# Attention sums with the tails added in, a small first transfer, and a new order table

## The chip, the cores and the metric

The kernel runs on one core of a Trainium2 chip. A core has a matrix engine (PE), three elementwise engines (DVE, ACT, POOL) and a queue engine (SP) that issues nearly all transfers; each executes its own list of instructions in order and waits for the others through semaphores. The metric is the device time of one execution in microseconds (us). Everything is float32 to the reference's accuracy, which is why one product is often made of three.

## The reference

Four batches of 12 heads, 448 positions, head size 64; then a gated block whose width is 768.

```python
scores = (q @ k.T) / 8
scores = cap * tanh(scores / cap)
attn   = softmax(scores)              # + 1e-9 in the denominator
x      = attn @ v                     # heads side by side: [4, 448, 768]
h      = gelu(x @ w_in)               # 768 -> 1024, tanh form
u, v   = h[..., :512], h[..., 512:]
v      = layernorm(v) * g_ln
v_s    = w_sg @ v + b_sg              # over the 448 positions
out    = x + (u * v_s) @ w_out        # 512 -> 768
```

## The kernel before

**Attention.** Two heads make a *pair* (24 pairs, 6 per batch, input pairs `q2[b, p]` and `k2[b, p]` of 128 rows by 448 columns), and two pairs make a *group* (12 groups, three per batch). The 448 keys are three chunks of 128 and a tail of 64. So a group has seven *units*: pair 0 with key chunks 1, 2, 3, pair 1 with chunks 1, 2, 3, and one unit that holds the tails of both pairs. One unit does, in this order:

- its scores on PE, for two heads at once. A chunk's scores (line 548) use the pair split in a high and a low half: `hl` is made by a cast (line 331 on DVE or 333 on ACT) and a subtraction (DVE, line 361), both 896 columns wide, and three products of the halves are added. The tail's scores (line 556) and the very first unit's (line 562, `whole`) take the raw float32 inputs and need no split;
- tanh and exp on ACT (lines 617 and 619, 896 columns each), in a tile `p`;
- values on PE (line 576, the tail's 586) into the pair's sums in PSUM;
- denominators: a matmul with columns of ones adds `p` over the keys into `den` (line 493, at most two units in one step). In a group whose entry in `SUMS` is 0 each of the seven units goes there. Where it is 1, DVE first adds the three chunks of a pair (line 636, 896 columns), so that two sums and the tail unit are left: three in place of seven.

Per batch a reciprocal follows through DRAM (lines 643 to 666), and the pairs' results are scaled and split again for the gated block.

**Gated block**, once per batch, on PE: `hv` (line 756, 18 matmuls for each 128 positions, three or four such blocks), `hu` (line 796, four blocks of 18), `vsg` (line 813, four blocks of 11), `outp` (line 834, six blocks of 12). Each block ends in one PSUM bank, and two banks at most are held by them at a time (`G_CAP`). The gelu of a block is Square on ACT (737), a step on DVE (739), Tanh on ACT (742), a step on DVE (744); the second step frees the bank.

**Weights** come as 64-bit numbers and are taken apart on DVE (lines 415 to 430), put together by POOL (line 435), then split in two halves (331 or 333, and 361). This is done for 12 chunks of `w_in` and 8 of `w_out`, and fills DVE early in the program.

**The order.** Nothing is ordered by hand. Each operation has a key from tables at the top (`ATT`, `GATED`, `IN_V`, `SPLIT`, `NORM`, ...), and `Plan.run` simulates five engines with fixed costs and takes, for each engine, the ready operation with the smallest key (a change of kind of matmul on PE is charged with `SWITCH`). Buffers are pools (`SIZES`). What comes out is a fixed list per engine.

Of the kernel before, what the change touches and what calls it, by code (L numbers as in the profile page):

```python
# [8 lines left out]
FP32 = mybir.dt.float32  # L9
# [13 lines left out]
ATT = ((-72.86, 2.67), (-7.76, 2.13), (126.82, 7.56), (80.49, -23.95))  # L23
GATED = ((141.52, 109.73), (434.23, 29.43), (324.93, 194.27), (407.54, 133.09))
SWITCH = 338.54
SIZES = (3, 6, 4, 4, 14, 2)
# [8 lines left out]
RETIRE = (12, 12, 11, 12, 0, 0)
IN_V = (418.5, 26.3)
IN_U = (73.7, 77.4)
OUT_W = (67.1, 53.5)
SG_W = (1690.2, 26.3)
FETCH_W = 222.3  # L40
FETCH_G = 41.72
SPLIT = 63.86
SG_FETCH = (349.8, 62.0)
GELU = 320.1
NORM = 231.27
RECIP = 518.42
VAL = 45.43
DEN = 46.86
DEC_AHEAD = 258.5
# [205 lines left out]
def kernel(  # L255
# [10 lines left out]
    consts: bass.AP,  # L266
    outT: bass.AP,
# [77 lines left out]
    k_const, k_bsg, k_g, k_pw = (Buf() for _ in range(4))  # L345
# [18 lines left out]
    load(lambda: const_sb, consts, k_const, 80000, -98.7)  # L364
# [8 lines left out]
    op("dve", 0.5, prepare, rd=[k_const], wr=[k_guard], key=1.0)  # L373
# [5 lines left out]
    def warm():  # L379

        z, o = Buf(p_p), Buf(ps_p, cls="w")
        op("dve", 0.3, lambda: nc.vector.memset(z.t[:, 0, :256], 0.0), wr=[z], key=-99.0)

        def fn():
            for _ in range(WARM):
                nc.tensor.matmul(
                    out=o.t[:, :256], lhsT=z.t[:, 0, :128], rhs=z.t[:, 0, :256], start=True, stop=True)
        op("pe", WARM * mms(4, 256, sets=1), fn, rd=[z], wr=[o], key=-99.0, mode="G")
# [91 lines left out]
    def attention(b):  # L480
# [3 lines left out]
        total = sum(3 if s else NU for s in SUMS[NG * b:NG * b + NG])  # L484
# [22 lines left out]
        def group(gi):  # L507
            g = NG * b + gi
            i0 = NU * g
# [21 lines left out]
            def split(s):  # L531
                key = akey(i0 + (FC + 1) * s) - SPLIT
                parts = range(2) if g == 0 and s == 0 else (slice(0, 2),)
                for n in parts:
                    cols = S if isinstance(n, int) else 2 * S
                    reg = n if isinstance(n, int) else None
                    cop(lambda n=n: hl[s].t[:, 0, n], lambda n=n: raw[s].t[:, n], cols,
                        [(raw[s], reg)], [(hl[s], ("h", n) if reg is not None else "h")], key)
                    sub(lambda n=n: hl[s].t[:, 1, n], lambda n=n: raw[s].t[:, n], lambda n=n: f32(hl[s].t[:, 0, n]), cols,
                        [(raw[s], reg), (hl[s], ("h", n) if reg is not None else "h")],  # L540
                        [(hl[s], ("l", n) if reg is not None else "l")], key)

            def scores(i, s, c, sc):
                def fn():
# [7 lines left out]
                def tail():  # L552
                    for s in range(2):
                        for h in range(2):
# [3 lines left out]
                                rhs=raw[s].t[rows, 0], start=True, stop=True, skip_group_check=True)  # L558
                def whole():
                    for h in range(2):  # L560
                        rows = slice(64 * h, 64 * h + 64)
                        nc.tensor.matmul(
                            out=sc.t[:, h, :S], lhsT=raw[s].t[rows, 1, 128 * c - 128:128 * c],
                            rhs=raw[s].t[rows, 0], start=True, stop=True)

                if c == 1 and s == 0 and not g:
# [370 lines left out]
```

## Time and profile before

| what | before |
|---|---|
| three runs | 391.77 us median (388.27 to 392.88) |
| the profiled execution | 390.62 us, of which the span of instructions is 388.2 us |
| PE busy | 377.8 us, 97% of the span |
| DVE busy | 288.4 us, 74% |
| ACT busy | 232.8 us, 60% |
| PE idle, or without work, at the two ends | until 4.0 us, and from 384.5 us |

The shares are averages. The first 109 us hold batches 0 and 1 of attention, the first units of batch 2 and the decoding of `w_in`; from there on the gated blocks alternate with the rest of attention; the last 112 us are gated work alone.

### The profile page before, as it was taken

The page shows a single profiled execution, that of the slowest core. Times are in us where ns is not written, and L with a number is a line of the kernel's source. Part 1 is how long each engine was busy: PE and PEld are TensorE (multiplying, and loading weights), DVE is VectorE, ACT ScalarE, POOL GpSimd, SP SyncE. Part 2 cuts the span into 40 slices and gives each one's busy share as a digit, 9 for nine tenths or more (in the row PEclk, how much of TensorE's full clock was granted, in tenths as well). Part 3 has the DMA queues.
Part 4 walks back from the last instruction along what each step waited for, and adds up shares of the span by engine and source line. Part 5 has one row for each costly group of instructions (what it writes and reads, how often), then busy time and mean ns, then how long its engine had stood idle before and what let it go on. Part 6 is the DMA issues. An engine that isn't in the chain of part 4 may idle for free.

```text
span 388.2 us, 5669 instructions
## 1 busy us (share of the span) xinstructions
PE 377.8 (97%) x2112; PEld 252.7 (65%) x2112; DVE 288.4 (74%) x521; ACT 232.8 (60%) x313; POOL 46.5 (12%) x38
## 2 busy tenths in 40 slices
PE   6998999999999999999999999999999999999996
PEld 3433433434788475888965844445689889889995
DVE  3699999799999999837656574878377797365642
ACT  5998999998456896714347399987134413133200
POOL 0261023046231310201000000000010000010000
PEclk9999999999999999999999999999999999999999
DMA  8981752864253533420004114322121201100012
GB/s 254 333 284 35 245 179 64 243 207 165 54 130 112 160 94 104 163 94 0 2 0 122 49 41 134 101 96 95 34 54 49 71 24 61 59 0 2 1 71 95
DMA packets 26155, 39.59 MB, mean 102 GB/s; under 512 B 5809, under 2 KB 23569, under 8 KB 26129
## 3 DMA queue, kind: packets, MB, share of 16 engines
q1 hardware_dynamic: 25984, 39.13, 32.0%
q8 instruction: 16, 0.26, 0.3%
q10 hardware_dynamic: 144, 0.11, 0.1%
q14 instruction: 11, 0.08, 0.1%
HBM read 33.21 MB, written 6.02 MB: 101 GB/s over the span
## 4 chain that ended last, share of the span: by engine, by line
PE 72%; DVE 15%; DMA 6%; ACT 2%; issue 2%; SPq 1%; POOL 0%; DVEq 0%; ACTq 0%; POOLq 0%
PE ps L796 11%; PE ps L576 10%; PE ps L756 9%; PE sc L548 8%; PE ps L834 8%; PE ps L813 6%; PE sc L834 4%; PE sc L796 4%; PE den L493 4%; PE sc L756 3%; DVE hl L361 2%; PE sc L813 2%; PE ps L586 2%; DMA n<-spread 2%; PE sc L556 2%
## 5 line engine op out<-in xcount | busy, mean ns | idle before, releaser
L617 ACT ACTIVATE p<-sc,qsc 128x896 f32<-128x896 f32 x84 | 81.3, 1019 | 10.7 <-DVE p L636 4.2
L619 ACT ACTIVATE p<-p,const_sb 128x896 f32<-128x896 f32 x84 | 84.0, 1059 | 0.1
L576 PE MATMUL ps<-p,v 128*64 128x448 f32 x288 | 61.2, 550 | 0.2 <-ACT p L619 0.2
L548 PEld LDWEIGHTS sc<-hl 64*128 64x128 f32 x426 | 35.9, 184 | 38.4 <-ACT p L617 19.8
L548 PE MATMUL sc<-hl 64*128 64x448 f32 x426 | 56.9, 388 | 2.8 <-ACT p L617 2.4
L435 POOL TENSOR_TENSOR stage<-stage 128x512 int32<-128x512 int32 (+1 forms) x20 | 38.3, 1918 | 112.5 <-DVE stage L430 111.1
L756 PE MATMUL ps<-win,rg 128*128 128x512 f32 x188 | 45.2, 395 | 0.0
L796 PE MATMUL ps<-rg,win 128*128 128x448 f32 x206 | 44.0, 365 | 0.0
L834 PE MATMUL ps<-rg,wout 128*128 128x448 f32 x184 | 43.4, 368 | 0.2
L636 DVE TENSOR_TENSOR p<-p,p 128x896 f32<-128x896 f32 x36 | 39.0, 1085 | 5.5 <-PE ps L576 3.1
L756 PEld LDWEIGHTS ps<-win,rg 128*128 128x128 f32 x188 | 35.3, 188 | 8.5
L796 PEld LDWEIGHTS ps<-rg,win 128*128 128x128 f32 x206 | 38.6, 187 | 3.4
L576 PEld LDWEIGHTS ps<-p,v 128*64 128x64 f32 x288 | 17.6, 136 | 34.2 <-issue 23.0
L834 PEld LDWEIGHTS ps<-rg,wout 128*128 128x128 f32 x184 | 34.0, 188 | 4.8 <-issue 0.9
L737 ACT ACTIVATE t<-ps 128x448 f32<-128x448 f32 (+1 forms) x23 | 13.1, 568 | 37.6 <-PE ps L756 22.5
L361 DVE TENSOR_TENSOR hl<-raw,hl 128x896 fp32r<-128x896 f32 (+1 forms) x25 | 26.8, 1070 | 6.1 <-ACT hl L333 5.9
L772 POOL TENSOR_TENSOR sm<-sm,pw 128x1 f32<-128x1 f32 x14 | 8.0, 572 | 189.9 <-DVE sm L769 189.9
L742 ACT ACTIVATE t<-t 128x448 f32<-128x448 f32 (+1 forms) x30 | 18.1, 603 | 16.4 <-DVE t L739 16.3
L813 PE MATMUL ps<-wsg,rg 128*128 128x448 f32 x116 | 26.3, 369 | 0.0
L739 DVE SCALAR_TENSOR_TENSOR t<-t,ps 128x448 f32<-128x448 f32 (+1 forms) x23 | 14.9, 647 | 14.0 <-ACT t L737 13.9
L493 PE MATMUL den<-p,const_sb 128*32 128x448 f32 x192 | 24.1, 549 | 0.3 <-DVE p L636 0.3
L813 PEld LDWEIGHTS ps<-wsg,rg 128*128 128x128 f32 x116 | 21.6, 188 | 3.0 <-issue 1.0
(114 smaller groups left out, 463.8 us busy)
## 6 DMA issues: line engine op xcount, KB each, us to landing
stage<-in_w_in_dram SPq DMA_DIRECT2D x12, 512.0 KB
raw<-in_q_dram SPq DMA_DIRECT2D x24, 224.0 KB
raw<-in_k_dram SPq DMA_DIRECT2D x24, 224.0 KB
n<-spread SPq DMA_DIRECT2D x24, 224.0 KB
out_dram<-x SPq DMA_DIRECT2D x23, 224.0 KB
v<-in_vp_dram SPq DMA_DIRECT2D x24, 192.0 KB
stage<-in_w_out_dram SPq DMA_DIRECT2D x8, 384.0 KB
u<-in_w_sgT_dram SPq DMA_DIRECT2D x4, 224.0 KB
```

What stands on the lines that cost most here:

```text
L361: op("dve", c_tt(n), lambda: nc.vector.tensor_tensor(out=out(), in0=a(), in1=b(), op=ALU.subtract), rd=rd, wr=wr, key=key, fast=True)
L435: nc.gpsimd.tensor_tensor(out=a.bitcast(I32), in0=a.bitcast(I32), in1=hi, op=ALU.add)
L493: nc.tensor.matmul(out=den.t[32 * j:32 * j + 32, :S], lhsT=ones_sb[:, kind, NP - 1 - kind - p:NP + 31 - kind - p], rhs=src.t[:, h, :], sta ...
L548: nc.tensor.matmul(out=sc.t[:, h, :S], lhsT=hl[s].t[rows, w, 1, 128 * c - 128:128 * c], rhs=hl[s].t[rows, m, 0], start=(k == 0), stop=(k = ...
L576: nc.tensor.matmul(out=pav[s].t[64 * h:64 * h + 64, :S], lhsT=v[s].t[:, 128 * (c - 1) + 64 * h:128 * (c - 1) + 64 * h + 64], rhs=p.t[:, h, ...
L617: op("act", c_act(2 * S, True, True), lambda p=p, sc=sc: nc.scalar.activation(out=p.t, in_=sc.t[:, :, :S], func=ACTF.Tanh, scale=qsc), rd= ...
L619: op("act", c_act(2 * S, False, True), lambda p=p: nc.scalar.activation(out=p.t, in_=p.t, func=ACTF.Exp, scale=cap_sb), rd=[k_const], wr=[ ...
L636: op("dve", c_tt(2 * S), lambda a=a, p=p: nc.vector.tensor_tensor(out=a.t, in0=a.t, in1=p.t, op=ALU.add), rd=[p], wr=[a], key=akey(i) + 5. ...
L756: nc.tensor.matmul(out=ps.t[:, :HF], lhsT=(xl if a else xh)[c].t[:, t * 128:t * 128 + 128], rhs=win[w][:, c, HF:], start=(c == 0 and k == ...
L796: nc.tensor.matmul(out=ps.t[:, :S], lhsT=win[w][:, c, f * 128:(f + 1) * 128], rhs=(xl if a else xh)[c].t[:, :S], start=(c == 0 and k == 0) ...
L813: nc.tensor.matmul(out=ps.t[:, :S], lhsT=(vl if a else vh)[c].t[:, f * 128:(f + 1) * 128], rhs=wsg[w][:, c, :], start=(c == 0 and k == 0), ...
L834: nc.tensor.matmul(out=ps.t[:, :S], lhsT=wout[w][:, f, c * 128:(c + 1) * 128], rhs=(gl if a else gh)[f].t[:, :S], start=(f == 0 and k == 0 ...
```

## The change

1. **Sums.** `SUMS` may now be 2: the halves of the tail unit's `p` (64 rows each) are added into the two pairs' sums on DVE, with two additions of 64 rows by 896 columns, and only two units go to `den`. The last four groups get 2; group 5 goes from 0 to 1. `TPOS` puts the tail unit second in each group (fourth in group 0).
2. **Plain pairs.** A table `PLAIN` names three pairs (0 and 3 of batch 0, 0 of batch 2) whose chunks' scores are made by `whole` from raw float32, without a split.
3. **First transfer.** A new input `first` holds 128 columns of k of the first pair, and `cap`; it is loaded ahead of all else, and the first unit reads its keys there. `const_sb` loses `cap` and is loaded later.
4. **Warm-up matmuls** at the start have 208 columns (`WCOLS`) in place of 256.
5. **Order.** New numbers in all key tables and costs; five `p` tiles in place of six and 16 `x` tiles in place of 14.

```diff
-ATT = ((-72.86, 2.67), (-7.76, 2.13), (126.82, 7.56), (80.49, -23.95))
+ATT = ((-54.55, 0.66), (20.94, 1.35), (147.45, 6.3), (106.98, -9.84))
-SIZES = (3, 6, 4, 4, 14, 2)
+SIZES = (3, 5, 4, 4, 16, 2)
...
-SUMS = (0, 1, 1, 1, 0, 0, 1, 1, 1, 1, 1, 1)
+SUMS = (0, 1, 1, 1, 0, 1, 1, 1, 2, 2, 2, 2)
+PLAIN = (1, 0, 0, 1, 0, 0, 0, 0, 0, 0, 0, 0, 1, 0, 0, 0, 0, 0, 0, 0, 0, 0, 0, 0)
...
-    load(lambda: const_sb, consts, k_const, 80000, -98.7)
+    load(lambda: first_sb, first, k_first, 70000, -99.5)
+    load(lambda: const_sb, consts, k_const, 60000, -98.3)
...
-        total = sum(3 if s else NU for s in SUMS[NG * b:NG * b + NG])
+        total = sum((NU, 3, 2)[s] for s in SUMS[NG * b:NG * b + NG])
...
+                if PLAIN[NP * b + pairs[s]]:
+                    return
...
-                if c == 1 and s == 0 and not g:
-                    op("pe", mms(4, sets=1), whole, rd=[raw[s]], wr=[sc], key=akey(i), mode="F")
+                if early:
+                    op("pe", mms(4, sets=1), whole, rd=[(raw[s], 0), k_first], wr=[sc], key=akey(i), mode="S")
+                elif c and PLAIN[NP * b + pairs[s]]:
+                    op("pe", mms(4, sets=1), whole, rd=[raw[s]], wr=[sc], key=akey(i), mode="S")
...
-            units.insert(FC if g else 1, (0, 0))
+            units.insert(tpos, (0, 0))
...
+                def add(a, p, rows=slice(0, 128)):
+                    op("dve", c_tt(2 * S), lambda: nc.vector.tensor_tensor(
+                        out=a.t[rows], in0=a.t[rows], in1=p.t[rows], op=ALU.add),
+                       rd=[p], wr=[a], key=akey(i) + 5.0, fast=True)
...
+                if SUMS[g] == 2 and (c == 0 or (s, c) == (1, 1)):
+                    add(per[s], tail_p, slice(64 * s, 64 * s + 64))
+                if (s, c) == ((0, 0) if SUMS[g] == 2 and tpos == FC else (0, FC)) or (s, c) == (1, FC):
+                    den_unit(pairs[s], 0, per[s], akey(i) + DEN, last)
```

**PE at the start.** Ahead of these rows stand only the warm-up matmuls. `sc` are the two score banks, `raw` the inputs of a pair, `hl` its halves, `ps` a pair's sums, `p` the exponentials. Before (line 562 is `whole`, 556 the tail's scores, 548 the scores from the halves, 576 values):

```order
L562 MATMUL sc_126<-raw_80 128x448 x2
L556 MATMUL sc_127<-raw_80 64x448 x2
L556 MATMUL sc_127<-raw_81 64x448 x2
L548 MATMUL sc_126<-hl_83 128x448 x6
L576 MATMUL ps_129<-p_91,v_85 64x448 x2
```

The same place of the change (571 is `whole`, 563 the tail's scores, 587 values, 501 denominators):

```order
L571 MATMUL sc_128<-raw_81,first_sb 128x448 x2
L571 MATMUL sc_129<-raw_81 128x448 x2
L571 MATMUL sc_128<-raw_81 128x448 x2
L563 MATMUL sc_129<-raw_81 64x448 x2
L563 MATMUL sc_129<-raw_82 64x448 x2
L587 MATMUL ps_131<-p_92,v_86 64x448 x2
```

The three chunks of pair 0 now come first, from raw inputs, and the tails, which need both pairs, fourth; the first product from halves has moved behind values and denominators.

**DVE at the gelus of the first gated block.** These are the rows up to the second step of the second `hv` block, which frees the bank that the first `hu` block takes. `t` is a gelu tile, `ps` the bank, `stage` a weight chunk being decoded, `win` the halves of `w_in`, `d` the reciprocals of batch 1. Before:

```order
L739 SCALAR_TENSOR_TENSOR t_117<-t_117,ps_130 128x512
L425 TENSOR_SCALAR stage_78<-stage_78 128x512
L430 SCALAR_TENSOR_TENSOR stage_78<-stage_78 128x512
L657 SCALAR_TENSOR_TENSOR d_139<-d_139,guard 64x84
L744 SCALAR_TENSOR_TENSOR t_118<-t_117,ps_130 128x512
L660 RECIPROCAL d_139<-d_139 64x84
...
L739 SCALAR_TENSOR_TENSOR t_115<-t_115,ps_128 128x512
L768 BN_AGGR sm_122<-sm_122 128x2
L361 TENSOR_TENSOR win_64<-stage_78,win_63 128x512
L769 TENSOR_SCALAR sm_122<-sm_122 128x1
L361 TENSOR_TENSOR wout_66<-stage_79,wout_65 128x384
L744 SCALAR_TENSOR_TENSOR t_116<-t_115,ps_128 128x512
```

And with the change (758 and 763 are the two gelu steps, 429 to 438 the decoding):

```order
L758 SCALAR_TENSOR_TENSOR t_119<-t_119,ps_131 128x512
L368 TENSOR_TENSOR win_64<-stage_80,win_63 128x512
L676 SCALAR_TENSOR_TENSOR d_141<-d_141,guard 64x84
L763 SCALAR_TENSOR_TENSOR t_120<-t_119,ps_131 128x512
...
L758 SCALAR_TENSOR_TENSOR t_117<-t_117,ps_132 128x512
L438 SCALAR_TENSOR_TENSOR stage_79<-stage_79 128x512
L793 TENSOR_SCALAR t_120<-t_120,sm_124 128x512
L763 SCALAR_TENSOR_TENSOR t_118<-t_117,ps_132 128x512
...
L368 TENSOR_TENSOR win_64<-stage_79,win_63 128x512
```

The last subtraction of a `w_in` chunk (stage_78 before, stage_79 now) stood ahead of that second gelu step and stands behind it now; the work on a `w_out` chunk has moved out of these rows.

**PE behind the first gated block's last `hv` block.** The last rows are the block's last matmul and what follows. Before, attention of batch 2 follows (its tails and a chunk):

```order
L756 MATMUL ps_128<-win_63,rg_700 128x512
L556 MATMUL sc_127<-raw_80 64x448 x2
L556 MATMUL sc_127<-raw_81 64x448 x2
L548 MATMUL sc_126<-hl_84 128x448 x6
```

With the change nine matmuls of `vsg` (line 832) come first, the last of which is the first row here:

```order
L832 MATMUL ps_130<-wsg_67,rg_628 128x448
L587 MATMUL ps_131<-p_94,v_86 64x448 x2
L555 MATMUL sc_129<-hl_84 128x448 x6
L555 MATMUL sc_128<-hl_84 128x448 x6
```

A block of `vsg` is now begun, left in its bank, and finished after ten units of attention.

## Rows read from the trace of the kernel before

**Rows 1.** Stretches: from:to, length, busy PE, PEld, DVE, ACT, POOL (instructions), clock, DMA, GB/s
```profile
4.00:8.60 4.60, 2.98 (x15) 0.77 (x14) 2.59 (x9) 2.41 (x5) 0.00 (x0) 1.00 1.01 330
...
13.50:108.90 95.40, 92.07 (x609) 41.34 (x601) 91.73 (x156) 85.28 (x100) 30.85 (x14) 1.00 0.56 177
108.90:170.10 61.20, 61.01 (x325) 45.56 (x326) 57.49 (x118) 41.13 (x65) 9.93 (x10) 1.00 0.42 129
```

**Rows 2.** Timeline of PE: start, length, line, operands, count [idle before <-releaser]
```profile
108.86 0.48 PE L796 MATMUL ps<-r,win 128*128 128x448 f32 x1 [0.33 <-DVE t L744]
```

**Rows 3.** The chain that ended last, at that place: start, length, what
```profile
108.12 0.70 DVE t L744
...
108.86 15.12 PE ps L796 x72
```

**Rows 4.** What DVE waited for between 13.4 and 108.9 us: total, times, longest
```profile
DVE x L699 <- DMA n<-spread: 2.5, 2, 1.9
DVE stage L421 <- DMA stage<-in_w_in_dram: 2.2, 3, 1.4
```

**Rows 5.** Timeline of DVE, two places where it works back to back
```profile
83.24 0.64 DVE L331 CAST hl<-raw 128x896 fp32r<-128x896 f32 x1
83.78 0.64 DVE L361 TENSOR_TENSOR rg<-x,rg 128x448 fp32r<-128x448 f32 x1
...
97.64 1.08 DVE L361 TENSOR_TENSOR hl<-raw,hl 128x896 fp32r<-128x896 f32 x1
98.65 0.68 DVE L361 TENSOR_TENSOR win<-stage,win 128x512 fp32r<-128x512 f32 x1
99.25 1.08 DVE L636 TENSOR_TENSOR p<-p,p 128x896 f32<-128x896 f32 x1
100.25 0.41 DVE L421 TENSOR_SCALAR stage<-stage 128x512 f32<-128x512 f32 x1
```

**Rows 6.** Timelines of ACT and DVE at the start
```profile
6.65 0.95 ACT L333 ACTIVATE hl<-raw 128x896 fp32r<-128x896 f32 x1 [1.36 <-DMA raw<-in_k_dram]
7.50 0.99 ACT L617 ACTIVATE p<-sc,qsc 128x896 f32<-128x896 f32 x1
...
13.48 0.45 DVE L421 TENSOR_SCALAR stage<-stage 128x512 f32<-128x512 f32 x1 [1.40 <-DMA stage<-in_w_in_dram]
```

**Rows 7.** Timeline of PE: the first unit, then attention back to back
```profile
4.04 1.02 PE L562 MATMUL sc<-raw 64*128 64x448 f32 x4
4.99 0.97 PE L556 MATMUL sc<-raw 64*64 64x448 f32 x4
...
41.18 1.72 PE L576 MATMUL ps<-p,v 128*64 128x448 f32 x8
42.84 1.48 PE L548 MATMUL sc<-hl 64*128 64x448 f32 x12
44.25 0.98 PE L586 MATMUL ps<-p,vt 64*64 64x448 f32 x8
...
47.49 2.48 PE L576 MATMUL ps<-p,v 128*64 128x448 f32 x12
49.90 0.87 PE L548 MATMUL sc<-hl 64*128 64x448 f32 x6
50.70 0.98 PE L556 MATMUL sc<-raw 64*64 64x448 f32 x8
51.61 1.72 PE L576 MATMUL ps<-p,v 128*64 128x448 f32 x8
...
70.79 1.71 PE L493 MATMUL den<-p,const_sb 128*32 128x448 f32 x16
72.43 0.88 PE L548 MATMUL sc<-hl 64*128 64x448 f32 x6
```

**Rows 8.** Timeline of POOL
```profile
83.13 9.17 POOL L435 TENSOR_TENSOR stage<-stage 128x512 int32<-128x512 int32 x1 [17.45 <-DVE stage L430]
...
103.28 1.29 POOL L435 TENSOR_TENSOR stage<-stage 128x512 int32<-128x512 int32 x1 [7.45 <-DVE stage L430]
```

More of the change, by code (lines that the diff above doesn't have):

```diff
@@ L31 @@
 WARM = 3
-COLD = 7.0
-SHARED = {'act': 224.0, 'dve': 104.5}
-SUMS = (0, 1, 1, 1, 0, 0, 1, 1, 1, 1, 1, 1)
[L35 to L49, printed above, removed]
+WCOLS = 208
+COLD = 4.1
+SHARED = {'act': 334.0, 'dve': 134.7}
+SUMS = (0, 1, 1, 1, 0, 1, 1, 1, 2, 2, 2, 2)
+PLAIN = (1, 0, 0, 1, 0, 0, 0, 0, 0, 0, 0, 0, 1, 0, 0, 0, 0, 0, 0, 0, 0, 0, 0, 0)
+RETIRE = (11, 12, 12, 12, 0, 3)
+IN_V = (90.12, 42.36)
+IN_U = (76.43, 52.83)
+OUT_W = (448.39, 25.57)
+SG_W = (2004.62, 22.75)
+FETCH_W = 142.75
+FETCH_G = 614.08
+SPLIT = 125.16
+SG_FETCH = (156.89, 59.95)
+GELU = 309.21
+NORM = 137.72
+RECIP = 888.07
+VAL = 24.89
+DEN = 12.46
+TVAL = 32.36
+TPOS = 1
+TPOS0 = 3
+DEC_AHEAD = 198.71
 ISSUE = 0.45
@@ L266 @@
     consts: bass.AP,
+    first: bass.AP,
     outT: bass.AP,
@@ L386, in fn @@
                 nc.tensor.matmul(
-                    out=o.t[:, :256], lhsT=z.t[:, 0, :128], rhs=z.t[:, 0, :256], start=True, stop=True)
-        op("pe", WARM * mms(4, 256, sets=1), fn, rd=[z], wr=[o], key=-99.0, mode="G")
+                    out=o.t[:, :WCOLS], lhsT=z.t[:, 0, :128], rhs=z.t[:, 0, :WCOLS], start=True, stop=True)
+        op("pe", WARM * mms(4, WCOLS, sets=1), fn, rd=[z], wr=[o], key=-99.0, mode="G")
     warm()
@@ L508, in group @@
             g = NG * b + gi
+            tpos = TPOS if g else TPOS0
             i0 = NU * g
@@ L532, in split @@
                 key = akey(i0 + (FC + 1) * s) - SPLIT
[L533 to L541, printed above, removed]
+                if PLAIN[NP * b + pairs[s]]:
+                    return
+                cop(lambda: hl[s].t[:, 0], lambda: raw[s].t, 2 * S, [raw[s]], [(hl[s], "h")], key)
+                sub(lambda: hl[s].t[:, 1], lambda: raw[s].t, lambda: f32(hl[s].t[:, 0]), 2 * S,
+                    [raw[s], (hl[s], "h")], [(hl[s], "l")], key)
             def scores(i, s, c, sc):
+                early = not g and not s and c == 1
                 def fn():
@@ L578, in fn @@
                             lhsT=v[s].t[:, 128 * (c - 1) + 64 * h:128 * (c - 1) + 64 * h + 64],
-                            rhs=p.t[:, h, :], start=(s == 0 and c == 1), stop=((s == 1 or not g) and c == FC),
+                            rhs=p.t[:, h, :], start=(s == 0 and c == 1), stop=((s == 1 or tpos < FC) and c == FC),
                             skip_group_check=True)
@@ L587, in tail @@
                                 out=pav[s].t[64 * h:64 * h + 64, :S], lhsT=vtail.t[rows, 64 * h:64 * h + 64],
-                                rhs=p.t[rows, h, :], start=(s == 1), stop=(g > 0 and s == 0), skip_group_check=True)
+                                rhs=p.t[rows, h, :], start=(s == 1), stop=(tpos == FC and s == 0), skip_group_check=True)
                 if c:
@@ L591, in values @@
                 else:
-                    op("pe", mms(4, sets=1, records=8), tail, rd=[vtail, p], wr=pav, key=akey(i) + VAL, mode="Q")
+                    op("pe", mms(4, sets=1, records=8), tail, rd=[vtail, p], wr=pav, key=akey(i) + TVAL, mode="Q")
             def evac(i, s):
@@ L877 @@
         plan.run()
-_INS = ["q2", "k2", "vp", "vt", "w_in", "w_sgT", "b_sg", "w_out", "consts"]
+_INS = ["q2", "k2", "vp", "vt", "w_in", "w_sgT", "b_sg", "w_out", "consts", "first"]
 def kernel(**inputs):
```

39 lines of the change are left out of this document (21 added, 18 removed).

## The prediction

> **What bounds the kernel now.** I read the page's busy times first (in the table above): PE 97%, DVE 74%. Neither number decides, so the next view is the table of stretches, cut where the program changes its work. From 13.5 to 108.9 us DVE is busy for 91.73 of 95.40 us and PE for 92.07 [rows 1]: two engines are full at once. In the 61 us behind it DVE still has 57.49 us of work, PE 61.01.
>
> Which of the two sets the pace is told by what PE waits for at the seam. The first `hu` block begins at 108.86 after an idle 0.33 us, released by DVE's second gelu step [rows 2], and the chain that ended last enters PE there, out of DVE (108.12, line 744), to run 15.12 us through 72 matmuls [rows 3]. So at 108.86, which I call the *gate*, DVE is late and PE waits. DVE's list of waits up to there holds only transfers, 2.5 us for the broadcast reciprocals and 2.2 us for weight chunks, 1.4 of it at the very start [rows 4]. I take it that DVE from its first weight chunk at 13.48 [rows 6] to the gate is a sum of instructions, with a few us of transfers and collisions that the change doesn't touch. Behind the gate I take PE to be the bound: it has 0.2 us idle in the next 61 [rows 1].
>
> The time is then: gate, plus PE's work behind it, plus the end.
>
> **What ends at the gate: DVE.** I counted the instructions of both orders from the first decoding step to that gelu step. A price is the distance between two starts where DVE works back to back [rows 5]: subtraction of 896 columns 1.01 us (97.64 to 98.65), of 512 columns 0.60, addition of 896 columns 1.00, cast of 896 columns 0.54 (83.24 to 83.78). Half widths I take at half, 0.5 and 0.3 (estimates).
>
> - Splits: 13 subtractions and 12 casts stood there, now 10 and 9. Three pairs are plain or already split before the first chunk lands: -3.0 and -1.6.
> - Additions: 14, now 16 (group 5 has moved to sums; none of the tails' additions is this early): +2.0.
> - `w_sg` is split ahead of the gate, three chunks more, each a cast and a subtraction of 448 columns: +2.4. The work on a `w_out` chunk has moved behind it (four instructions of 384 columns, three quarters of 0.60 twice and of some 0.35 twice): -1.4. The last `w_in` subtraction has moved behind it: -0.6. A layernorm step and a cast come ahead: +0.8.
>
> Sum -1.4 us. The start of that work doesn't gain: DVE waits for the first chunk of `w_in` [rows 6], and 66 KB more now go ahead of it, at 330 GB/s [rows 1] +0.2. So the gate moves from 108.9 to 107.7, **-1.2**.
>
> **What the first transfer gains, and why I cost it at nothing.** Before, the first scores end near 5.0 [rows 7], but tanh starts at 7.50, because ACT had first to wait for the second pair's k until 6.65, and to cast it [rows 6]. The new order has no cast on ACT there, and the first scores need only the small table and one q: tanh can begin near 5.1, 2.4 us earlier. That puts ACT and PE ahead, and DVE's decoding is the cover that hides it: both arrive at the gate and wait. If DVE were not the bound it would be worth the whole 2.4 (first rival). The shorter warm-up, three matmuls of 48 columns less, is hidden in the same way.
>
> **What is left behind the gate: PE.** Prices, again from start to start [rows 7]: one more unit of values 0.75 (four records more: 1.66, then 2.41 us), entering values 0.16; a unit of chunk scores 0.61 and entering it 0.20 (1.41 for two, 0.80 for one); a tail's scores 0.91; two steps of denominators 1.64, so 0.75 for a step of two units and 0.14 to enter. The first unit took 0.95 with raw inputs against 0.80 with halves, so a plain unit costs 0.15 more; eight more of them are 1.2 us, all ahead of the gate, where PE waits anyway.
>
> Behind the gate the orders differ so: denominators 36 matmuls, now 28 (four units, two steps): -1.5. One chunk's scores -0.6 and one tail's scores -0.9, which now lie ahead of it; one unit of values more, +0.75. Changes of kind: values entered 18 times instead of 14 (+0.6), scores 20 instead of 22 (-0.4), denominators 7 instead of 8 (-0.1), gated kinds five times more, for which I have no clean row: between nothing and the 0.20 of scores, I take 0.1 (+0.5). Sum **-1.7**; with the ends of the unknown -2.2 to -1.2.
>
> The eight additions of 64 rows and four more of 128 lie on DVE mostly behind the gate. No row shows 64 rows by 896 columns; bounds are nothing and the 1.00 of 128 rows, and I take 1.00, since an instruction's length here follows its columns. PE hides them, if DVE keeps up: in the next stretch 23 units of attention now stand beside the first gated block's second half, where 11 stood, and DVE had 3.7 us to spare in 61. I leave this at nothing, with up to 3 us of new waits in the range.
>
> **Sum.** 388.2 - 1.2 - 1.7 = 385.3 us of span; 2.4 us lie around the span, so the profiled execution would be 387.7 in place of 390.62. The median of the runs shown stands 1.15 us above that execution, which gives 388.9. I predict 388.5.
>
> **Rivals.**
>
> *The start carries through* (chance 0.17). If DVE's waits for transfers vanish because denominators and reciprocals come earlier, PE decides. Its work ahead of the gate is 1.0 us more (eight raw units at 0.75 for seven from halves at 0.61, one tail unit more, two steps of denominators and one unit of values less, some changes of kind). It starts 2.4 earlier, and of the 3.3 us that it idled in that stretch (95.40 - 92.07) [rows 1] none need stay: the gate is at 104.2. Span 388.2 - 4.7 - 1.7 = 381.8, time 384.2 on the profiled execution's scale. For it: DVE waited 3.7 us in this stretch. Against it: the new list puts the same distance of work between the reciprocals and their first use.
>
> *A late chunk of `w_in`* (chance 0.10), the side on which it gets slower. The last chunk's decoding now ends about 1.1 us ahead of the gate, and its subtraction has moved behind the gate. POOL's step stands between: usually 1.29 us, but once 9.17 [rows 8]. With 1.3, a cast and the subtraction, the halves are there some 1.5 us behind the gate; `hu` asks for them after 15 matmuls, 3.2 us behind it at 0.2 each [rows 3]. So it decides from 3.0 us of POOL on. At 9.2 PE stands 6.2 us: span 391.5, time 393.9. For it: the long one ran while DVE went through subtractions and multiplications of two inputs, and such stand there now. The Trainium skill (GPSIMD Engine Reference, 1. Specifications) says why it could be so: POOL's memory interfaces are shared with VectorE, and DVE instructions with two SBUF inputs contend with it. By that rule each of this change's additions is a chance to hold POOL up; the 9.17 us agree, the 1.29 us beside other additions don't make it regular. Against it: before, even the 9 us cost PE nothing.
>
> *Nothing happens* (chance 0.13). What PE saves at denominators it waits for at additions, or DVE's order loses in collisions what its sum gains: 390.6 to 391.8.
>
> The forecast has the remaining 0.60.
>
> **Range and chances.** The unknowns of the forecast (1 us in the changes of kind, 3 of new waits, 2 or 3 of transfers and collisions) make it 386 to 391. Eight in ten needs the upper half of the first rival and nothing: 383.5 to 392.5. About 2% is what a measurement of this kernel can tell from no change, since three runs lie 1.2% apart. Faster by over 2% is below 383.9: half of the first rival and a little of the forecast, 0.11. Slower by over 2% is above 399.6, which no single mechanism here reaches: 0.02.
>
> **What would show it.** Tanh starts at 5.0 to 5.5 in place of 7.50. DVE's first decoding step stays within 0.5 us of 13.5. PE shows more waiting than before between 13 us and the gate, on DVE, and the first `hu` block begins at 107 to 108.5. From there to the last matmul PE takes about 274 us (275.6 before: 384.5 - 108.9). Were the gate below 105, DVE was no bound and the first rival holds; were it at 108 but the stretch behind it longer than 276, the additions have turned into waits; an idle PE some 3 us into the first `hu` block is the late chunk.

## The result, and the profile after

The changed kernel takes 385.91 us (median of 20 runs, 384.68 to 389.13) where the kernel before took 389.54 (387.67 to 392.88) on the same chip: a ratio of 0.9897, with a 95% interval of 0.9874 to 0.992. The prediction was 388.5 us with a range of 383.5 to 392.5, and no change beyond 2%. The profiled execution has a span of 383.6 us, before 388.2: 4.6 us less, where the prediction summed 2.9.

The busy times, from the profile's page:

```profile
PE 373.9 (97%) x2064; PEld 250.7 (65%) x2064; DVE 298.9 (78%) x533; ACT 229.7 (60%) x305; POOL 44.4 (12%) x38
```

PE has 3.9 us less to do than before, DVE 10.5 us more. The stretches, which answer to [rows 1] (from:to, length, busy PE, PEld, DVE, ACT, POOL, clock, DMA, GB/s), cut at the first `hu` block again:

```profile
4.00:8.60 4.60, 4.16 (x18) 1.49 (x20) 0.13 (x1) 3.18 (x4) 0.00 (x0) 1.00 0.97 307
13.50:108.80 95.30, 92.55 (x581) 39.89 (x580) 92.22 (x154) 85.57 (x97) 26.59 (x13) 1.00 0.59 187
108.80:170.10 61.30, 60.38 (x355) 39.41 (x355) 60.75 (x120) 44.68 (x66) 9.26 (x10) 1.00 0.36 111
```

PE works earlier at the start, and yet the middle stretch has kept its length. The timelines of ACT, DVE and PE at the places of [rows 6] and [rows 2]:

```profile
5.42 1.91 ACT L628 ACTIVATE p<-sc,qsc 128x896 f32<-128x896 f32 x2 [1.82 <-PE sc L571]
...
13.66 0.43 DVE L429 TENSOR_SCALAR stage<-stage 128x512 f32<-128x512 f32 x1 [1.95 <-DMA stage<-in_w_in_dram]
...
105.11 3.83 PE L775 MATMUL ps<-win,rg 128*128 128x512 f32 x16
108.78 0.37 PE L815 MATMUL ps<-r,win 128*128 128x448 f32 x1
...
112.75 0.48 PE L815 MATMUL ps<-rg,win 128*128 128x448 f32 x1 [0.37 <-DVE win L368]
```

Tanh starts 2.1 us earlier; the gate (the first `hu` block) stands at 108.78, before at 108.86. PE no longer waits there: its row has no idle time in front of it and follows the matmuls of `hv` (line 775). Four us behind the gate PE waits 0.37 us for the last chunk of `w_in`. The chain that ended last, which in [rows 3] entered PE at the gate, now enters it at this second place, out of DVE:

```profile
108.85 0.70 DVE sm L786
110.73 0.60 DVE t L758
111.33 1.38 DVE win L368
112.75 11.40 PE ps L815 x55
```

What DVE waited for ahead of the gate answers to [rows 4]:

```profile
DVE stage L429 <- DMA stage<-in_w_in_dram: 2.3, 2, 1.9
DVE x L718 <- DMA n<-spread: 1.7, 2, 1.6
```

So the time came from behind the gate. From the first `hu` matmul to the end of the last matmul it was 275.6 us before, and is 271.2 now. Summed over PE's timeline, each group of matmuls from its start to the next group's start, this stretch gained 2.8 us in denominators (9.07 to 6.23), 1.1 in chunk scores, 0.9 in tail scores, 0.9 in `hv` (46.33 to 45.41) and 0.5 in `outp` (60.22 to 59.71), and lost 2.0 in values (28.44 to 30.40), of which 0.55 is a wait for one of DVE's additions; the other kinds differ by 0.2 or less each.

### The profile page after: what moved, and what is told of

It is laid out like the page before. It is cut to its first block, busy times and chain, and to the rows that moved or that the text cites. A ratio compares the mean times of both kernels' runs of the same rounds, so it can differ in the third digit from the quotient of the medians.

```text
span 383.6 us, 5583 instructions
## 1 busy us (share of the span) xinstructions
PE 373.9 (97%) x2064; PEld 250.7 (65%) x2064; DVE 298.9 (78%) x533; ACT 229.7 (60%) x305; POOL 44.4 (12%) x38
## 4 chain that ended last, share of the span: by engine, by line
PE 55%; DVE 22%; ACT 9%; DMA 7%; issue 4%; SPq 1%; POOL 1%; DVEq 0%; ACTq 0%
PE ps L815 12%; PE ps L775 11%; PE ps L853 7%; DVE p L640 6%; PE sc L853 5%; ACT p L628 5%; PE ps L587 4%; ACT p L630 4%; PE ps L832 3%; PE sc L832 3%; PE sc L555 3%; PE sc L815 3%; DMA n<-spread 2%; DVE hl L368 2%; DMA raw<-in_k_dram 2%
## 5 line engine op out<-in xcount | busy, mean ns | idle before, releaser
L630 ACT ACTIVATE p<-p,first_sb 128x896 f32<-128x896 f32 x84 | 83.5, 1045 | 0.1
L640 DVE TENSOR_TENSOR p<-p,p 128x896 f32<-128x896 f32 (+1 forms) x48 | 52.8, 1100 | 10.1 <-ACT p L630 6.0
L775 PE MATMUL ps<-win,rg 128*128 128x512 f32 x223 | 52.7, 392 | 0.0
L555 PE MATMUL sc<-hl 64*128 64x448 f32 x378 | 50.5, 389 | 1.4 <-ACT p L628 1.4
L775 PEld LDWEIGHTS ps<-win,rg 128*128 128x128 f32 x223 | 41.9, 188 | 9.0
L756 ACT ACTIVATE t<-ps 128x512 f32<-128x512 f32 (+1 forms) x26 | 14.8, 570 | 44.4 <-PE ps L775 27.9
L853 PE MATMUL ps<-rg,wout 128*128 128x448 f32 x167 | 38.3, 367 | 0.2 <-DVE wout L368 0.2
L758 DVE SCALAR_TENSOR_TENSOR t<-t,ps 128x512 f32<-128x512 f32 (+1 forms) x26 | 16.9, 650 | 17.2 <-ACT t L756 17.1
L368 DVE TENSOR_TENSOR hl<-raw,hl 128x896 fp32r<-128x896 f32 x21 | 23.1, 1102 | 0.0
L853 PE MATMUL sc<-rg,wout 128*128 128x448 f32 x97 | 22.7, 364 | 0.0
```

The lines of the kernel that those rows point to most:

```text
L368: op("dve", c_tt(n), lambda: nc.vector.tensor_tensor(out=out(), in0=a(), in1=b(), op=ALU.subtract), rd=rd, wr=wr, key=key, fast=True)
L555: nc.tensor.matmul(out=sc.t[:, h, :S], lhsT=hl[s].t[rows, w, 1, 128 * c - 128:128 * c], rhs=hl[s].t[rows, m, 0], start=(k == 0), stop=(k = ...
L630: op("act", c_act(2 * S, False, True), lambda p=p: nc.scalar.activation(out=p.t, in_=p.t, func=ACTF.Exp, scale=cap_sb), rd=[k_first], wr=[ ...
L640: op("dve", c_tt(2 * S), lambda: nc.vector.tensor_tensor(out=a.t[rows], in0=a.t[rows], in1=p.t[rows], op=ALU.add), rd=[p], wr=[a], key=ake ...
L775: nc.tensor.matmul(out=ps.t[:, :HF], lhsT=(xl if a else xh)[c].t[:, t * 128:t * 128 + 128], rhs=win[w][:, c, HF:], start=(c == 0 and k == ...
L853: nc.tensor.matmul(out=ps.t[:, :S], lhsT=wout[w][:, f, c * 128:(c + 1) * 128], rhs=(gl if a else gh)[f].t[:, :S], start=(f == 0 and k == 0 ...
```

## Which prices belong to one execution

The kernel before, traced once more.

> The kernel before once more, unchanged, for a second trace of it. Question: of the 4.4 us that the changed kernel saves from its first hu block on, some 1.5 us lie not in counts of matmuls but in their price (hv 0.2335 us each before, 0.2291 after). Theory A (the price differs from execution to execution): this trace shows hv prices anywhere from 0.229 to 0.234 and a stretch from the first hu block to the last matmul that is up to 1.5 us off 275.5. Theory B (the price belongs to the order): hv is 0.233 to 0.234 again and the stretch 275.2 to 275.8 us. The gate (first hu block) should be at 108.6 to 109.1 in both. Time ratio 1.00.

Ratio 1.001 (0.9984 to 1.0036). The stretch behind the gate is 275.49 us for 275.64, `hv` in it 46.28 for 46.33, denominators 9.05 for 9.07: theory B, these belong to the order. The gate, expected at 108.6 to 109.1, does not: it stands at 109.75. PE had stood for 2.07 us here, and then worked at a clock of 0.50 for some us. PE's rows at that place and one stretch (in the columns of [rows 1]), then the same matmuls in the first trace:

```profile
32.37 1.05 PE L548 MATMUL sc<-hl 64*128 64x448 f32 x6 [2.07 <-ACT p L617]
...
37.30 1.50 PE L548 MATMUL sc<-hl 64*128 64x448 f32 x12
...
33.00:36.00 3.00, 3.00 (x16) 0.68 (x14) 3.00 (x6) 2.97 (x4) 1.42 (x1) 0.50 0.00 0
```

```profile
32.06 0.88 PE L548 MATMUL sc<-hl 64*128 64x448 f32 x6 [1.52 <-ACT p L617]
...
35.41 1.48 PE L548 MATMUL sc<-hl 64*128 64x448 f32 x12
```

From the first row to the second it is 4.93 us for 3.35: the slower clock cost PE 1.6 us, more than the 0.9 by which the gate is late. In the table of all traces, the numbers are DVE's first decoding instruction, PE's first `hu` matmul, their distance, and the stretch from there to PE's last matmul:

| trace | decoding starts | gate | distance | behind the gate |
|---|---|---|---|---|
| before | 13.48 | 108.86 | 95.4 | 275.6 |
| before, again | 13.83 | 109.75 | 95.9 | 275.5 |
| after | 13.66 | 108.78 | 95.1 | 271.2 |
| doubled denominators | 11.82 | 106.97 | 95.2 | 276.3 |
| units on the same columns | 14.97 | 109.21 | 94.2 | 274.8 |
| half additions | 12.51 | 106.84 | 94.3 | 271.6 |
| tanh at 6.34 | 14.06 | 108.64 | 94.6 | 274.4 |
| tanh at 7.36 | 12.95 | 107.71 | 94.8 | 273.2 |
| tanh at 9.55 | 12.46 | 111.10 | 98.6 | 272.6 |
| early chunk | 12.02 | 107.54 | 95.5 | 272.6 |
| and early subtraction | 11.63 | 108.19 | 96.6 | 271.5 |
| and second chunk | 11.54 | 105.95 | 94.4 | 272.3 |
| sums, tails in none | 12.30 | 109.33 | 97.0 | re-ordered |
| sums, tails in six | 12.14 | 106.75 | 94.6 | re-ordered |

A granted clock of 0.50 ahead of the gate stands only in the rows "before, again" and "tanh at 9.55". The gate tends to follow DVE's start, but loosely: a start at 12.30 has it at 109.33, one at 13.66 at 108.78. And the stretch behind the gate belongs to the order less than the first two rows suggest: the eight traces with the same matmuls there as the changed kernel (all but the first two rows, the two with altered denominators and the two re-ordered ones) take 271.2 to 274.4 us, 272.4 on average. The traced 271.2 is the shortest, so the gain behind the gate is 3.1 us on average, not 4.4. Part of the spread is PE's waits for DVE, 1.4 to 3.6 us there; the kernel before has none.

## Ahead of the gate: DVE and PE

**Half of the additions away.**

```diff
+                    n = 1 if g < 6 else 2
-                        out=a.t[rows], in0=a.t[rows], in1=p.t[rows], op=ALU.add),
+                        out=a.t[rows, :n], in0=a.t[rows, :n], in1=p.t[rows, :n], op=ALU.add),
```

> The changed kernel, with the additions into the sums of groups 0 to 5 done for one head's 448 columns only; the other head's additions are left out, so that its denominators there are wrong. It takes about 16 times 0.47 = 7.5 us of DVE's work away, nearly all of it ahead of the first hu block, and nothing of any other engine. Theory A (DVE is the bound there): the gate moves from 108.78 to where PE becomes the bound, 103.5 to 105, and the time by -4 to -5 us, to about 381.5. Theory B (PE or ACT sets the gate, DVE only keeps up): the gate moves by less than 1 us, time 385 to 386. In both, the stretch behind the gate stays at 271.2 within 0.5 us.

384.47 us, ratio 0.9839 (0.9793 to 0.9885). An addition of half the columns takes 720 ns, not half of 1,103. The stretch from 13.5 us to the gate in this kernel:

```profile
13.50:106.84 93.34, 92.22 (x582) 40.21 (x581) 84.59 (x152) 85.33 (x97) 20.71 (x13) 1.00 0.60 192
```

From its first decoding step to the second gelu step of the second `hv` block DVE is busy for 85.16 us, where the changed kernel has 91.54: 6.4 us less. But the distance from its start to the gate shrinks by 0.8 only (95.1 to 94.3); the rest of the earlier gate is an earlier start. PE is now busy in 92.22 of 93.34 us, and with all additions in place the gate stands as early in three other traces (105.95, 106.75 and 106.97 in the table). Theory A is out; the distance moves as theory B has it, and the time lies between the two. PE is as full there as DVE was, and by the distance DVE's relief is worth about 1 us. The stretch behind the gate stayed (271.6), as expected.

**The start's gain taken back**, by 24, 12 or 16 idle activations on ACT ahead of the first tanh:

```diff
+    def late():
+        nc.scalar.activation(out=guard, in_=guard, func=ACTF.Exp)
+        for _ in range(24):
+            nc.scalar.activation(out=idle, in_=first_sb[:, :32], func=ACTF.Copy)
```

> The changed kernel, with 24 short activations on ACT ahead of the first tanh, so that tanh starts about 2 us later than its 5.42 us: it takes the start's gain away and nothing else. Theory A (up to the first hu block DVE is the bound, from its first chunk of w_in at 13.66 on): the gate stays within 0.5 us of 108.78 and the time within 0 to +0.5 us of the changed kernel's 385.9. Theory B (the start carries through: the gain of 2.1 us at tanh is part of what the change brought): the gate and the time move by +1.5 to +2.1 us, to 387.4 to 388.0.

They delayed tanh by 4.1 us, twice what was meant: it starts at 9.55. 388.61 us, ratio 0.9953 (0.9925 to 0.9981), 2.2 us above the changed kernel's ratio, and the distance to the gate is 98.6 us. But a late tanh is not all that this kernel has. PE stood for 3.76 us, and then its clock was 0.50:

```profile
10.59 1.87 PE L577 MATMUL sc<-raw 64*128 64x448 f32 x4 [3.76 <-ACT p L634]
12.39 1.77 PE L569 MATMUL sc<-raw 64*64 64x448 f32 x8
14.09 2.95 PE L593 MATMUL ps<-p,v 128*64 128x448 f32 x8
...
17.86 1.49 PE L561 MATMUL sc<-hl 64*128 64x448 f32 x12
...
10.00:16.00 6.00, 5.41 (x18) 1.58 (x20) 4.46 (x9) 5.94 (x7) 1.29 (x1) 0.50 0.93 307
```

With 16 activations (below) the clock stays at 1.00, and the same matmuls take 4.55 us for 7.27:

```profile
8.40 1.02 PE L577 MATMUL sc<-raw 64*128 64x448 f32 x4 [1.17 <-ACT p L634]
...
12.95 1.49 PE L561 MATMUL sc<-hl 64*128 64x448 f32 x12
```

So 2.7 us of PE's delay come from the clock, as much as the whole loss in time, and this run can't tell how late a tanh DVE's decoding would cover. Two smaller delays were to find it:

> The changed kernel with 12 of the short activations ahead of the first tanh in place of 24, so that tanh starts at about 7.5 us, where it started before the change: exactly the start's gain is taken away. With 24 of them (tanh at 9.55) DVE took 98.6 us from its first chunk of w_in to the first hu block, and 95.2 without. Theory A (DVE's decoding covers a delay of some 2 us, and more than that comes through): 95.2 to 95.8 us, time 385.9 to 386.5. Theory B (the chain from the first tanh is at the bound as well, with about 0.6 us to spare): 96.5 to 97.0 us, time 386.9 to 387.5, so that the start's gain is worth 1 to 1.5 us of the change.

> The changed kernel with 16 of the short activations ahead of the first tanh, since 12 put it at 6.34 us only and 24 at 9.55: it should start at 7.4, as before the change (7.50). Tanh at 6.34 cost nothing (385.97 us), tanh at 9.55 2.7 us. Theory A (the first 2 us are covered by DVE's decoding): 385.7 to 386.5 us. Theory B (the chain from the first tanh has less than 1 us to spare): 386.8 to 387.4.

With 12, tanh started at 6.34 us and the time was 385.97, ratio 0.9905 (0.9874 to 0.9935): no loss. With 16 it started at 7.36 us, as before the change; ratio 0.9927 (0.9896 to 0.9958), 1.2 us above the changed kernel's ratio with about 1.5 of uncertainty. The distance to the gate is 94.8 us in that trace, no longer than in the changed kernel. The trace speaks for theory A, the median for some loss; what the start's gain is worth stays between 0 and some 2.7 us.

**The first chunk of `w_in` earlier.** The order of all else is kept; its transfer goes past two transfers of tails and two of v. 

```diff
+        chunk0 = next(x for x in sp if x[1].key == round(IN_V[0] - FETCH_W, 6))
+        emit.remove(chunk0)
+        emit.insert(emit.index(sp[9]), chunk0)
```

> The changed kernel with one transfer moved: the first chunk of w_in is issued ahead of both tails of v and two of v's transfers in place of behind them (384 + 128 KB), all else in the same order. It should land about 1.5 us and its issue come 1.9 us earlier, so DVE starts decoding at 10.9 to 11.5 us in place of 11.8 to 13.7. Theory A (the gate is DVE's start plus 95.2 us): the first hu block starts at 106 to 106.8, the time falls by 1 to 2 us, to 384 to 385. Theory B (PE has work up to 106.5 to 107 anyway, as where VectorE had only half the additions): the gate stays at 106.5 to 107.2 however early the chunk comes, the time falls by 0 to 0.8 us. Theory C (the values wait for the transfers that now come later): PE waits more in its first 15 us, and the time is the same or longer.

384.84 us, ratio 0.9858 (0.9821 to 0.9896), 1.5 us below the changed kernel's ratio (the intervals overlap). DVE starts at 12.02 and now waits 1.29 us at 15.0 for the second chunk; the gate is at 107.54. The gate lies above the ranges of both theories A and B, since DVE started later than expected, and the time fits A by the medians (1.1 us) without ruling out B. Theory C is out: no wait of PE for v is in the trace, and those for k and q ahead of the gate are 0.8 and 0.4 us, where the changed kernel has 0.4 and 0.3.

```diff
+        chunk1 = next(x for x in sp if x[1].key == round(IN_V[0] + IN_V[1] - FETCH_W, 6))
+        emit.remove(chunk1)
+        emit.insert(emit.index(sp[10]), chunk1)
```

> The kernel with the early chunk and the early subtraction, with the second chunk of w_in issued earlier too, ahead of one tail of v and two of v's transfers. With the first chunk alone moved, DVE started decoding at 12.02 but waited 1.29 us for the second chunk at 15.0. Theory A (DVE's start decides up to the first hu block): the gate and the time fall by another 0.5 to 1.2 us, to 383 to 383.7. Theory B (PE is as full as DVE by now, its waits ahead of the gate were 2.7 us): 0 to -0.3 us. Theory C (the values wait for v): the same or up to 1 us longer.

With the second chunk earlier too (and the subtraction below) the time is 383.36 us, ratio 0.9818 (0.9763 to 0.9873). DVE no longer waits for `w_in`, and the gate, at 105.95, is the earliest of all. But with its six runs (381.66 to 385.89) it can't be told from the kernel without that step (0.9828).

## Behind the gate: PE, and the last chunk of `w_in`

**Denominators doubled.**

```diff
-                for half, (p, kind, src) in enumerate(units):
+                for half, (p, kind, src) in list(enumerate(units)) * (2 if b > 1 else 1):
```

> The changed kernel, with every denominators matmul of batches 2 and 3 issued twice, so that their denominators come out doubled. These are seven steps, all behind the first hu block. Theory A (behind the gate PE is the bound, and a step of denominators costs by its matmuls): the stretch behind the gate grows by 7 times 0.75 = 5.3 us (271.2 to 276.5), the time to 391.2. Theory B (a step costs mostly for being entered: a step of one unit took 0.88 us, one of two units 0.89): the growth is well below 0.75 for a step that had one unit only, and in all 3.5 to 5 us. Theory C (other engines' lateness hides PE's work there): less than 2 us.

389.87 us, ratio 1.0004 (0.9971 to 1.0037). Behind the gate the denominators take 11.48 us for 6.23, the stretch 276.3 for 271.2: 5.1 us, theory A. Nothing hides PE's work there, but for the 0.55 us that PE had waited for an addition.

**Both units on the same columns.**

```diff
-                        j = 2 * half + h
+                        j = h if b > 1 and n0 else 2 * half + h
```

> The changed kernel, order unchanged, but in five of the seven steps of denominators behind the first hu block both units write the same 64 columns of the sums, where they wrote 64 columns each; the two halves are added later, so the result is the same. Theory A (the two units of a step run at the same time because they use different columns of the array, so a step costs the same with one unit or two): each of the five steps grows from 0.89 to about 1.64 us, the denominators there from 6.2 to 10.0 us, the time by 3.5 to 3.9 us, to about 389.6. Theory B (each unit costs 0.375 us wherever it goes, as the prediction priced it): no change, 385.9.

388.35 us, ratio 0.9942 (0.9908 to 0.9976). One step, first in the changed kernel, then with both units on the same columns, and the next group's start:

```profile
178.75 0.96 PE L501 MATMUL den<-p,const_sb 128*32 128x448 f32 x8
179.64 1.59 PE L555 MATMUL sc<-hl 64*128 64x448 f32 x12
```

```profile
180.70 1.70 PE L501 MATMUL den<-p,const_sb 128*32 128x448 f32 x8
182.32 1.50 PE L555 MATMUL sc<-hl 64*128 64x448 f32 x12
```

0.89 us becomes 1.62, and the denominators behind the gate 9.90 us for 6.23: 0.73 for each of the five, theory A. The two units of a step run side by side, so a step with one unit costs as much as a step with two. The kernel before shows such a step, with four records, beside a full one:

```profile
237.72 0.95 PE L493 MATMUL den<-p,const_sb 128*32 128x448 f32 x4
238.60 0.88 PE L548 MATMUL sc<-hl 64*128 64x448 f32 x6
...
240.22 0.96 PE L493 MATMUL den<-p,const_sb 128*32 128x448 f32 x8
241.12 0.88 PE L548 MATMUL sc<-hl 64*128 64x448 f32 x6
```

0.88 us and 0.90. The Trainium skill (TensorE: Matmul & The Clock Gate, Why this matters for your kernels) says that narrow matmuls run at the same time if each writes its own group of 32 output partitions; these runs agree.

The timed difference, 1.8 us by the ratios and 2.4 by the medians, with an uncertainty of some 1.6, is smaller than the 3.7 of the trace; why is open.

**The subtraction of the last chunk moved up**, past two instructions on DVE, on top of the early first chunk.

```diff
+        sub = next(x for x in dve if x[1].key == round(IN_U[0] + 5 * IN_U[1], 6) and len(x[1].engs) == 1)
+        emit.remove(sub)
+        emit.insert(emit.index(dve[dve.index(sub) - 2]), sub)
```

> The changed kernel with the first chunk of w_in issued early (384.84 us by itself) and one VectorE instruction moved: the subtraction of the last chunk of w_in goes two places up, ahead of a decoding step of w_out and a gelu step. It stood at 111.24 in the changed kernel, took 1.46 us because it ran beside a GpSimd addition, and PE waited 0.4 to 1.9 us for it in five traces. Theory A (that wait is on the path): no wait of PE on win behind the gate, and the time falls by another 0.4 to 0.8 us, to 384.0 to 384.4. Theory B (PE then waits for the gelu step or the w_out chunk that now come later): the time stays at 384.6 to 385.2.

DVE and POOL in the changed kernel, where it stood, then in this one:

```profile
111.24 1.46 DVE L368 TENSOR_TENSOR win<-stage,win 128x512 fp32r<-128x512 f32 x1
...
111.11 1.04 POOL L443 TENSOR_TENSOR stage<-stage 128x384 int32<-128x384 int32 x1
```

```profile
110.01 0.68 DVE L379 TENSOR_TENSOR win<-stage,win 128x512 fp32r<-128x512 f32 x1
...
111.30 1.03 POOL L454 TENSOR_TENSOR stage<-stage 128x384 int32<-128x384 int32 x1 [0.19 <-issue]
```

Started 0.13 us behind POOL's addition, the subtraction takes 1.46 us; clear of it, 0.68. PE's wait for `win` is gone (0.4 to 1.9 us in the ten traces where the subtraction stood behind them). 383.27 us, ratio 0.9828 (0.9781 to 0.9875); the median fell by 1.6 us against the early chunk alone, but the ratios differ by 0.3% with intervals of 0.4 to 0.5%, so what it is worth in time is not settled. The Trainium skill (SBUF — State Buffer, Who interferes with whom) says that a DVE instruction with two SBUF inputs contends with a GpSimd one that reads SBUF, that the port pair is an exclusive lock, and that issue order decides who blocks; the row at 111.24 agrees. The long POOL step of [rows 8] does not: by the profile it began at 83.13, and DVE's subtraction at 83.78 [rows 5], begun behind it, took 0.64 us and was not held up.

These two kernels are the fastest measured: 0.9818 and 0.9828 of the kernel before, where the change alone has 0.9897.

## One line of the change by itself

Two kernels alter `SUMS` alone, and let the planner order the rest.

```diff
-SUMS = (0, 1, 1, 1, 0, 1, 1, 1, 2, 2, 2, 2)
+SUMS = (0, 1, 1, 1, 0, 1, 1, 1, 1, 1, 1, 1)
```

> The changed kernel with its last four groups summed as the others are: the tails aren't added into the sums, so batches 2 and 3 have 9 and 9 units of denominators in place of 8 and 6, and VectorE has eight additions of 64 rows less. Up to the last steps ahead of the gated block of batch 1 the order on all engines is that of the changed kernel. Theory A (a step costs 0.89 us, whether it holds one unit or two: 10 steps for 7 behind the first hu block): denominators there take 8.9 us for 6.2, the stretch from the first hu block to the last matmul grows from 271.2 to 273.5 to 274.0, the time by about 2.6 us to 388.5. Theory B (a unit costs 0.375 and a step 0.14, as the prediction priced them): +1.9 us for four units and three steps. Theory C (the additions cost PE waits behind the gate, and they go too): less than +1.5.

```diff
-SUMS = (0, 1, 1, 1, 0, 1, 1, 1, 2, 2, 2, 2)
+SUMS = (0, 1, 1, 1, 0, 1, 2, 2, 2, 2, 2, 2)
```

> The changed kernel with the tails added into the sums in all six groups of batches 2 and 3 in place of four: batch 2 has 6 units of denominators for 8, so one step less behind the first hu block, and VectorE has four additions of 64 rows (1.09 us each) more there. Theory A (behind the first hu block PE is the bound and a step costs 0.89 us, the additions are hidden): the stretch falls from 271.2 to 270.2 to 270.6, the time by 0.7 to 1.0 us. Theory B (the additions come out as waits): the stretch is 271 to 273, the time the same or up to 2 us longer.

Nothing of this came: 410.89 us (ratio 1.0538) and 407.15 (1.043). Up to the gate the orders are the same; behind it the planner laid the gated work otherwise. In the first, PE has done all of it that it may when attention ends, and nothing is left to lay beside the last reciprocals:

```profile
306.39 0.94 PE L501 MATMUL den<-p,const_sb 128*32 128x448 f32 x4 [0.42 <-DVE p L640]
320.74 2.93 PE L775 MATMUL ps<-win,rg 128*128 128x512 f32 x6 [13.40 <-ACT rg L340]
```

DVE waits 6.5 us for the transfer to `d` and 6.3 for the one to `n`. The stretches of this kernel around the hole, in the columns of [rows 1]:

```profile
300.00:306.00 6.00, 4.68 (x24) 0.97 (x20) 3.59 (x4) 4.20 (x5) 0.00 (x0) 1.00 0.00 0
306.00:312.00 6.00, 0.94 (x4) 0.14 (x4) 0.34 (x1) 1.09 (x2) 0.00 (x0) 0.78 0.04 9
312.00:318.00 6.00, 0.00 (x0) 0.00 (x0) 0.97 (x2) 0.00 (x0) 0.00 (x0) 0.50 0.10 21
318.00:324.00 6.00, 3.26 (x8) 2.65 (x9) 2.20 (x10) 1.19 (x5) 0.00 (x0) 0.50 0.26 70
324.00:330.00 6.00, 6.00 (x25) 5.08 (x24) 1.90 (x5) 1.20 (x4) 0.00 (x0) 0.80 0.36 115
```

In the second kernel it is another place: from 230 to 280 us attention stands with little gated work beside it and PE waits for ACT's tanh and exp (busy 44.81 of 50 us).

```profile
230.00:280.00 50.00, 44.81 (x269) 22.32 (x270) 32.33 (x42) 33.12 (x38) 0.00 (x0) 1.00 0.33 100
```

Behind the gate PE's waits add up to 19.9 us in the first kernel and 16.2 in the second, where the changed kernel has 1.4. That is most of the 24.8 and 24.4 us by which this stretch grew; for the rest the traces show a lower clock around the holes (0.79 on average from 300 to 340 us in the first, 0.87 from 150 to 190 in the second), and how much that costs was not worked out.

So the order weights and `SUMS` are one change: the two other `SUMS` that were tried cost 21 and 25 us. What the new sums bring without an order made for them could not be told apart this way.

## Why the prediction was right, and where its sizes were off

**The gate is DVE's.** Right for the kernel before, not for the changed one. In the changed kernel PE doesn't wait at the gate in any of the twelve traces, and the second gelu step of the second `hv` block does not free the bank that the first `hu` block takes, though the section on the change says so of both orders. With tanh at 6.34 the block starts 1.9 us before that step (line 769) ends:

```profile
108.64 0.37 PE L821 MATMUL ps<-r,win 128*128 128x448 f32 x1
...
109.88 0.68 DVE L769 SCALAR_TENSOR_TENSOR t<-t,ps 128x512 f32<-128x512 f32 x1
```

Nor did PE wait more than before between 13 us and the gate, one of the signs named: it idles for 2.75 us (95.30 - 92.55), where it had 3.33. DVE still holds PE up ahead of the gate, by additions that come late for denominators or for ACT. These are two of the changed kernel's waits there (total, times, longest), and ACT, in the second, had itself waited 1.79 us for an addition:

```profile
PE den L501 <- DVE p L640: 0.8, 2, 0.5
PE sc L555 <- ACT p L628: 1.4, 1, 1.4
```

But the last wait for an addition ends between 65 and 94 us in the twelve traces, and from there PE runs without one up to the gate. What the prediction had too far away is PE: it put PE's gate at 104.2, and with DVE relieved of 6.4 us it stood at 106.8. So a saving of 6.4 us on DVE was worth about 1 us there.

**The sum, -1.4 us ahead of the gate.** Its terms came. Priced from start to next start in the two traces, the subtractions of 896 columns changed by -2.9 us, the casts by -2.3, the additions by +2.7, `w_sg` by +2.5, the `w_out` chunk by -1.7, the last `w_in` subtraction by -0.5, the layernorm step and the cast by +0.8: -1.4 together. But it was taken for granted that all else stays, and it grew by 2.0: the step on `b_sg` from 0.30 us to 1.44, which ran beside a POOL addition, the two steps that guard the reciprocals by 0.6, the decoding steps by 0.3. So DVE is busy for 91.54 us from its first decoding step to that gelu step, where it was 90.97. The distance to the gate fell by 0.3 in this pair; over the ten traces with all of the changed kernel's work ahead of the gate and tanh up to 7.4 us it averages 95.2, over the two of before 95.65, one of which had the slower clock. This is the step that failed ahead of the gate: -1.2 was forecast there, and it was -0.1.

**The first chunk "within 0.5 us of 13.5", +0.2.** In the traced pair it came as forecast, 13.66 for 13.48. As a sign it is no good: with the same transfers ahead of it the chunk started at 11.8 to 15.0 in the other traces. Between 11.82 and 14.97 the gate moved by 2.2 us (106.97 to 109.21); how much of the 4.4 us by which the changed kernel's 20 runs differ comes from it is not shown.

**The start costed at nothing.** Tanh began at 5.42 as forecast. Up to a tanh at 6.34 the gain is hidden, as said; whether 7.36 costs something is open, and at 9.55 the clock fell, so that the run can't say.

**Behind the gate, -1.7.** It was -4.4 in the traced pair and -3.1 on average: the mis-sized term. Denominators were priced by units (four units, two steps: -1.5, and -0.1 for entering); the order before had ten steps there, two of them with one unit, and the new one seven full ones. A lone unit costs a whole step, so three steps went, 2.8 us. Scores, with their entries, came as forecast (-1.0 and -0.9, measured -1.1 and -0.9), and so did values, 1.4 for 1.35 without the wait. `hv`, 0.9 us cheaper in all (about 0.229 us a matmul for 0.2335, in every trace of the one order and of the other where the clock stayed at 1.00), stood in no term, and its cause stays open. The other gated kinds, priced at +0.5 for being entered more often, took 0.7 us less.

**The additions hidden at nothing.** Nearly right. One of 64 rows takes 1.09 us, one of 128 rows 1.10, so the upper bound was the one; DVE is busy for 60.75 of the first 61.30 us behind the gate, and PE waits for an addition only once there, 0.55 us. Its waits for other late work of DVE make it 1.4 us behind the gate, and up to 3.6 in other traces; the range had 3 for them.

**The rivals.** "The start carries through" did not decide: the gate didn't move, though PE sets it now. Its sum left PE 1.0 us more work ahead of the gate; it was 2.0 (99.64 to 101.67 us busy from the first scores on), and of the 3.3 us of idle time 2.75 stayed. "A late chunk" was there in small: POOL's step took 1.55 us, not 9.2, and it was DVE's own subtraction that a second POOL addition held up; PE waited 0.4 us, not 6.2. Its reading of [rows 8] was off: of the twelve steps of `w_in` one took 9.17 us and the others 1.29 to 3.70, six of them over 1.6, and the one of 1.29 ran beside no addition of DVE's. Nor is 9.17 a matter of chance, since the kernel before, traced again, has it at the same step. "Nothing happens" was refuted by the stretch behind the gate.

**Luck.** In the traced pair -1.2 came as -0.1 and -1.7 as -4.4. The two errors have opposite signs and partly cancel in the sum, 2.9 us for 4.6 in that pair (3.6 by the medians, 4.0 by the ratio). The base worked the other way: 391.77 of the runs shown was above the 389.54 of the same kernel beside the changed one, so the forecast ended 2.6 us too high though its gain fell short by only some 0.7.

## What to carry to other kernels

Price narrow matmuls by the steps in which they run side by side, not by their number: a lone one costs a full step, so count odd ones. When two engines are busy for 92 of 95 us each, a saving on one is worth only its distance to the other, here about 1 us for 6.4 us saved; look for gains where one engine alone is the bound. And where a table makes the order, change an input of it only with the table: `SUMS` altered by itself cost 5.4 and 6.5% of the changed kernel's time. And where a run puts in a delay, look at the clock behind it before the loss is put down to the delay.

## What the runs showed of the hardware

- Two denominators matmul pairs on different groups of 32 columns run in 0.89 us, on the same ones in 1.62; one pair alone takes 0.88.
- After PE had stood for 3.76 us the granted clock was 0.50 (1.2 GHz) from 10 to 16 us, and matmuls that take 4.55 us at 1.00 took 7.27; after it had stood for 2.07 us in another trace, it was 0.50 from 33 to 36 us, and 3.35 us of matmuls took 4.93.
- After PE had stood since 307.3 us the granted clock was 0.50 (1.2 GHz) from 312 to 324 us, and 0.80 on average in the next 6 us, in which PE worked without a gap.
- The same transfer, issued at 7.5 to 7.8 us behind the same others, let DVE start at 11.8 us in one execution and at 13.66 in another.
- A subtraction of 512 columns took 1.46 us beside a POOL addition and 0.68 clear of it; an addition of 448 columns took 0.72 us, one of 896 columns 1.10.
